# From batch 3 on, q and k of a head on 64 partitions instead of 32: loaded twice, one element apart

## The chip, the cores and the metric

The kernel runs on one NeuronCore of a Trainium2 chip. The metric is the device time of one execution in microseconds (us), lower is better. A core has five engines that run their own instruction streams: TensorE (PE, matmuls; PEld is its weight load), VectorE (DVE), ScalarE (ACT), GpSimd (POOL) and SyncE (SP). Transfers are issued from an engine's queue (here SP, POOL and once ACT) and carried out by 16 DMA engines.

## The reference

Inputs are q, k and v of shape (8, 8, 576, 64) (batch, head, position, head dimension), and two weight matrices, (512, 2048) and (2048, 512), all float32.

```python
def _attn_ref(q, k, v):
    factor, Sd, scale = 4, S // 4, 1.0 / np.sqrt(D)
    # pooled part: means over 4 positions, full softmax attention over 144 positions
    q_d, k_d, v_d = (t.reshape(B, H, Sd, 4, D).mean(axis=3) for t in (q, k, v))
    out_up = np.repeat(softmax(scale * q_d @ k_d.T) @ v_d, 4, axis=2)
    # local part: only |i - j| < 4
    mask = np.abs(pos[:, None] - pos[None, :]) < 4
    out_local = softmax(np.where(mask, scale * q @ k.T, -1e9)) @ v
    return out_up + out_local

def _moe_ref(x, w_in, w_out):            # x: 4608 tokens x 512
    h = x @ w_in
    return (h * sigmoid(1.702 * h)) @ w_out
```

The two parts of attention are added, the heads are laid side by side as 512 columns, and the result passes through the two matrix products with the activation between them.

## The kernel before

**Tiling.** The 4608 tokens are cut into 9 groups of 512 (`n_groups`). For a group g, `mm1` computes 16 blocks of 128 hidden units (`ffc`), each of four 512-column matmuls over the model dimension (`dmc`, one for each pair of heads; L806), followed by an activation on ScalarE (L817). `mm2` computes four blocks of 128 tokens, 16 matmuls of 512 columns each (L884), followed by a copy on ScalarE and a store (L869, L874). So a group has 64 + 64 large matmuls.

**Order.** The schedule is written by hand: each engine runs its instructions in program order. The attention of batch b = g + 1 is threaded into the matmuls of group g. `attention(b)` returns five steps, and `POS` says before which matmul each is put: numbers below 16 are blocks of mm1, later ones are matmuls of mm2 counted from 16. The steps are: the scores of quad 0 on TensorE, their exponentials and masks, the scores and exponentials of quad 1, and twice attn-times-v (`avx`) for four heads.

**Scores.** A quad is four heads. `load_1` loads q or k of a quad as 128 partitions x 1152 bf16 values (the DMA, issued on GpSimd, casts from float32); two buffers per name and quad (`bufs=2`). `prep_1` (L312) transposes in blocks of 32x32 on VectorE, with two bf16 values taken as one float32. So a head lies on 32 partitions, and its 64 dimensions are 32 pairs (index `a`). A score is the sum of two matmuls with 32 rows, a = 0 and a = 1, accumulated in PSUM. `scores_mixed` issues per quad 80 local matmuls (L439: 64 keys by 60 queries) and 24 pooled ones through `scores_d` (L466: 64 keys by 144 queries), four at a time on the four row groups, on tiles of 32 rows by 64 columns. The pooled q and k (`qdT`, `kdT`) are sums of four positions: on GpSimd (`pool_qk`, two adds each, L343 and L347) or on VectorE (`reduce_qk`, one reduction, L331). Scores go to PSUM tiles PA (three of two banks each), exponentials to `es` and `ed` (L477, L503), and the local ones are multiplied by the band mask on VectorE (L511).

**The rest of attention.** `avx` works on 64x64 tiles, four abreast: L674 pooled, L696 local, each with denominators from a matrix of ones. ScalarE takes logarithms and an exponential for the reciprocal (L739 to L745), VectorE multiplies (L750), and the pooled part is added to xT on GpSimd for heads 0 to 3 and on VectorE for heads 4 to 7 (L766).

**Around it, per group.** Before mm1 of group g (batch b = g + 1, b below 8) this is issued; every engine picks out its own part:

```python
            load_v4(b)              # SP: v as rows of four positions, 12 transfers
            prep_qk(b, 0)           # DVE: transposes k and q of quad 0
            pool_qk(b, 0)           # POOL: their pooled sums
            if b + 1 < B:
                for qd in range(NQ):
                    load_qk(b + 1, qd)   # POOL queue: four loads
            prep_v(b, nc.gpsimd)    # POOL: v to bf16 (L353)
            if b + 1 < B:
                load_v(b + 1)       # SP: ten transfers
            prep_qk(b, 1)           # DVE: quad 1
            ...
            prep_v4(b, nc.gpsimd)   # POOL: pooled v (L360, L363), from v4 to vd
```

In the place of the dots quad 1's pooled sums are made, for b = 2 on VectorE and for later batches on GpSimd. Batch 0 is done ahead of the groups with its own functions (`scores0`, `normalise0`, `transp_sum`), and batch 1 in group 0.

## Time and profile before

| | us |
|---|---|
| median of 3 runs (313.42 to 315.02) | 314.03 |
| the profiled execution, its own time | 312.69 |
| its span, from first to last instruction | 310.9 |
| TensorE busy | 299.7 |
| ScalarE busy | 203.4 |
| VectorE busy | 148.3 |
| GpSimd busy | 146.9 |
| local score matmuls L439, 1120 of them, mean 0.195 each | 15.4 busy |
| pooled score matmuls L466, 384 of them, mean 0.237 each | 12.3 busy |
| transposes L312, 32 of 128x576, mean 1.24 each | 39.7 busy |

The granted TensorE clock is 1.00 over the span. Busy time of an engine is the union of its instructions' time. Small matmuls overlap on TensorE, so their mean durations say little of what they cost: the distance between starts does. Some matmul records are missing from a trace, which shows as a gap of twice the usual distance. A line such as L439 is the line of the kernel before; "idle before" names what the engine waited for.

### The profile page before, as it was taken

What the parts mean: (1) busy time and instruction counts of PE and PEld (TensorE: products, weight loads), DVE (VectorE), ACT (ScalarE), POOL (GpSimd) and SP (SyncE); (2) the same over time, 40 slices, a digit from 0 to 9 for tenths busy, and PEclk for the clock granted to TensorE, in tenths of its full rate; (3) what the DMA queues carried; (4) which work ended last, traced back from release to release, by engine and by line L of the source; (5) the groups of instructions that cost most, each with busy time, mean ns of one, the idle gap of its engine ahead of it and who ended that gap; (6) DMA issues with size and microseconds to landing.
All of it is one profiled execution on the core that took longest, in us unless ns stands there. A gap on an engine that the chain in (4) does not pass through costs nothing.

```text
span 310.9 us, 9597 instructions
## 1 busy us (share of the span) xinstructions
PE 299.7 (96%) x4138; PEld 156.2 (50%) x4181; DVE 148.3 (48%) x304; ACT 203.4 (65%) x327; POOL 146.9 (47%) x169
## 2 busy tenths in 40 slices
PE   8899999999999999999999999999999999999995
PEld 3464555665544464455545554555455544444444
DVE  6984936851694159505970499038902760000000
ACT  4755766777858786768866885589558857216511
POOL 8542393394229933894369634983396110000000
PEclk9999999999999999999999999999999999999999
DMA  6999999899527942795159705981430110010011
GB/s 110 138 208 209 185 136 216 241 201 226 161 94 163 206 120 87 166 224 139 70 168 201 177 36 174 193 211 39 137 89 34 39 70 0 34 67 36 0 67 67
DMA packets 64042, 39.93 MB, mean 128 GB/s; under 512 B 44544, under 2 KB 54912, under 8 KB 64000
## 3 DMA queue, kind: packets, MB, share of 16 engines
q0 software_dynamic: 18784, 14.94, 32.9%
q1 hardware_dynamic: 45072, 24.32, 28.0%
q8 instruction: 32, 0.52, 0.7%
q14 instruction: 10, 0.08, 0.1%
q10 hardware_dynamic: 144, 0.07, 0.1%
HBM read 44.81 MB, written 9.44 MB: 174 GB/s over the span
## 4 chain that ended last, share of the span: by engine, by line
PE 91%; DMA 2%; issue 2%; POOL 2%; ACT 1%; DVE 1%; POOLq 0%; DVEq 0%; ACTq 0%
PE pm L884 36%; PE pm L806 24%; PE pa L806 16%; PE pa L439 3%; DMA vb<-in_v_dram 2%; PE pa L884 2%; PE pa L696 2%; PE pa L674 2%; PE pa L466 2%; PE pm L899 1%; POOL vb L260 1%; PE pa L609 1%; PE pa L567 1%; PE pa L597 0%; POOL kb L218 0%
## 5 line engine op out<-in xcount | busy, mean ns | idle before, releaser
L884 PE MATMUL pm<-w_out_bf,gT 128*128 128x512 bf16 x503 | 114.6, 379 | 3.4 <-issue 3.2
L806 PEld LDWEIGHTS <-w_in_bf 128*128 128x128 bf16 x603 | 58.3, 98 | 63.8 <-issue 0.3
L806 PE MATMUL pm<-xT,w_in_bf 128*128 128x512 bf16 (+1 forms) x342 | 86.9, 375 | 0.6
L884 PEld LDWEIGHTS <-gT 128*128 128x128 bf16 x560 | 52.7, 98 | 62.4 <-issue 0.6
L817 ACT ACTIVATE gT<-pm 128x512 bf16<-128x512 f32 x88 | 52.7, 603 | 41.0 <-PE pm L806 41.0
L806 PE MATMUL pa<-xT,w_in_bf 128*128 128x512 bf16 (+1 forms) x245 | 59.0, 361 | 0.3
L511 DVE TENSOR_TENSOR es<-es,mask 128x600 bf16<-128x600 bf16 x28 | 17.2, 651 | 85.6 <-ACT es L477 85.5
L869 ACT ACTIVATE osb<-pm 128x512 f32<-128x512 f32 (+2 forms) x35 | 20.3, 583 | 30.5 <-PE pm L884 25.1
L817 ACT ACTIVATE gT<-pa 128x512 bf16<-128x512 f32 x56 | 32.1, 608 | 6.3 <-PE pa L806 6.3
L766 POOL TENSOR_TENSOR xT<-xT,od 128x576 bf16<-128x576 bf16 x12 | 15.4, 1280 | 40.0 <-DVE xT L750 40.0
L750 DVE TENSOR_TENSOR xT<-n,l 128x285 bf16<-128x285 f32 (+1 forms) x96 | 28.1, 366 | 0.0
L343 POOL TENSOR_TENSOR pq<-kT 128x576 f32<-128x576 bf16 x11 | 12.8, 1160 | 30.4 <-DVE kT L312 30.4
L871 DVE TENSOR_SCALAR osb<-pm 128x128 f32<-128x128 f32 x1 | 0.3, 291 | 53.8 <-ACT osb L869 53.8
L360 POOL TENSOR_TENSOR pq<-v 112x512 f32<-112x512 f32 x18 | 23.7, 1317 | 3.9 <-DMA v<-in_v_dram 3.9
L312 DVE STREAM_TRANSPOSE kT<-kb 128x576 f32<-128x576 f32 x16 | 19.9, 1244 | 4.4 <-DMA kb<-in_k_dram 4.4
L312 DVE STREAM_TRANSPOSE qT<-qb 128x576 f32<-128x576 f32 x16 | 19.8, 1238 | 0.3
L503 ACT ACTIVATE ed<-pa 128x864 bf16<-128x864 f32 x16 | 14.3, 894 | 7.2 <-PE pa L466 7.2
L477 ACT ACTIVATE es<-pa 128x600 bf16<-128x600 f32 x28 | 17.2, 669 | 0.1
L745 ACT ACTIVATE l<-l 128x1440 f32<-128x1440 f32 x12 | 16.8, 1404 | 0.4
L740 DVE COPY n<-pa 128x492 f32<-128x492 f32 x24 | 15.0, 665 | 2.7 <-ACT l L739 2.0
L739 ACT ACTIVATE l<-pa 128x492 f32<-128x492 f32 x24 | 12.6, 578 | 4.6 <-PE pa L696 3.7
L439 PE MATMUL pa<-qT,kT 32*64 32x60 bf16 x1120 | 15.4, 195 | 0.0
(132 smaller groups left out, 355.0 us busy)
## 6 DMA issues: line engine op xcount, KB each, us to landing
out_dram<-osb SPq DMA_DIRECT2D x34, 256.0 KB, 2.2
vf<-in_v_dram SPq DMA_DIRECT2D x60, 128.0 KB, 4.9
v<-in_v_dram SPq DMA_DIRECT2D x72, 96.0 KB, 3.1
kb<-in_k_dram POOLq DMA_DIRECT2D x16, 288.0 KB, 6.5
qb<-in_q_dram POOLq DMA_DIRECT2D x16, 288.0 KB, 8.6
w_out_bf<-in_moe_w_out_dram POOLq DMA_DIRECT2D x4, 512.0 KB, 13.2
w_in_bf<-in_moe_w_in_dram POOLq DMA_DIRECT2D x2, 512.0 KB, 6.8
w_in_bf<-in_moe_w_in_dram POOLq DMA_DIRECT2D x1, 1024.0 KB, 12.2
```

What stands on the lines that cost most here:

```text
L312: nc.vector.transpose(out=t32.rearrange("p (i c) -> p c i", c=18), in_=store[b, qd].bitcast(FP32).rearrange("p (c d) -> p c d", c=18),)
L360: eng.tensor_tensor(out=t1[0:112], in0=x[:, :, 0:2, :], in1=x[:, :, 2:4, :], op=ALU.add)
L439: nc.tensor.matmul(P[1 + r // 2][64 * par : 64 * par + 64, r % 2, 60 * i : 60 * i + 60], lhsT=kT[b, qd][rows, k0 : k0 + 64, a], rhs=qT[b, ...
L477: nc.scalar.activation(out=es[2 * qd + u][:, :, 0:300], in_=sp[u][:, :, 0:300], func=AF.Exp, scale=inv_sqrt_d,)
L511: nc.vector.tensor_tensor(out=ev, in0=ev, in1=mask, op=ALU.mult)
L745: nc.scalar.activation(out=l, in_=l, func=AF.Exp, scale=-1.0)
L750: nc.vector.tensor_tensor(out=out, in0=sub(n, *part), in1=sub(l, *part), op=ALU.mult)
L766: eng.tensor_tensor(out=xs, in0=xs, in1=sub(od[:, u, :], 0, (1, SD), (0, 4)), op=ALU.add)
L806: nc.tensor.matmul(acc[:, c : c + n], lhsT=w_in_bf[:, dmc, ffc * 128 : (ffc + 1) * 128], rhs=xT[dmc][:, g * TG + c : g * TG + c + n], star ...
L817: nc.scalar.activation(out=gT[:, ffc, :], in_=acc, func=AF.Silu, scale=GELU_SCALE)
L869: eng.activation(out=osb, in_=ap, func=AF.Copy, scale=1.0 / GELU_SCALE)
L884: nc.tensor.matmul(ops[t], lhsT=gT[:, ffc, t * 128 : (t + 1) * 128], rhs=w_out_bf[:, ffc, :], start=(ffc == 0), stop=(ffc == n_ffc - 1),)
```

## The change

From batch 3 on (`WIDE = 3`) the four heads of a quad are taken as two pairs u, each on 64 partitions. The 2 x 576 x 64 values of a pair are 32 rows of 2304. A load puts them on 32 partitions, and once more on the next 32, beginning one element later (so 2303 values each). The transposition by float32 pairs is the same operation, with 36 instead of 18 blocks per row. Of every pair only its first value is used: the first copy gives the even dimensions, the second the odd ones. So a head's 64 dimensions lie on 64 partitions, a score is one matmul of 64 rows, on 64x64 tiles (`scores_wide`), and a quad has 40 local and 12 pooled matmuls.

With it come: one raw tile of 2304 columns per name and quad, whose halves serve as the two buffers of the batches before 3, and which is a single buffer from batch 3 on; tiles of twice the length for the transposed q and k, in whose second halves batch 0's y and the helper dm0 lie; the pooled sums of quad 1 on VectorE in every batch from 2 on; the loads of quad 1 issued after `prep_v4`; steps 3 to 5 of the attention one matmul later; and in group 8 eight matmuls of 512 columns issued as two of 256.

```diff
...
     n_dmc = d_model // 128
     n_ffc = d_ff // 128
     n_groups = B * S // TG
+    WIDE = 3
     inv_sqrt_d = 1.0 / math.sqrt(D)
     KSTART = (0, 56)
     QSTART = (0, 60)
...
         ez.append(t[:, 0:2560].rearrange("p (u j i c) -> p u j i c", u=2, j=2, c=128))
     v4 = persist.tile([128, 3, HP, 4 * D], FP32, name="v4")
     kdT = [persist.tile([128, 160, 2], BF16, name=f"kdT{i}") for i in range(NQ)]
+    raw = {
+        (n, qd): persist.tile([128, 2304], BF16, name=f"{n}b{qd}")
+        for qd in range(NQ) for n in "kq"
+    }
 
     PA = [psum.tile([128, 2, 512], FP32, name=f"pa{i}") for i in range(3)]
     PM = [psum.tile([128, 512], FP32, name=f"pm{i}") for i in range(2)]
...
     PSEL_AT = {(i, kc): 48 * kc - 114 * i // 4 + (EVEN + 37 if i % 2 else 18)
                for i, kc in ((0, 0), (1, 0), (1, 1), (2, 1), (3, 1), (3, 2), (4, 2))}
 
-    dm0 = consts.tile([128, Q0], FP32, name="dm0")
     dm = consts.tile([128, 60], FP32, name="dm")
     di = consts.tile([128, 128], FP32, name="di")
     dr = consts.tile([128, 1], FP32, name="dr")
...
         for t in ez:
             nc.vector.memset(t.rearrange("p u j i c -> p (u j i) c")[:, :, Q0:128], 1.0)
         for t in kT0:
-            nc.vector.memset(t[:, S:, :], 0.0)
+            nc.vector.memset(t[:, S : S + 8, :], 0.0)
         nc.vector.memset(vbs[0][96:128, 4, :, 0:D], 0.0)
         make_bias()
         make_off()
...
     qf, kf, vf = {}, {}, {}
 
     def load_1(name, src, store, b, qd):
-        t = ldp.tile(
-            [128, 1152], BF16, name=f"{name}b{qd}", tag=f"{name}b{qd}", bufs=2
-        )
+        t = raw[name, qd]
+        if b >= WIDE:
+            store[b, qd] = t
+            for u in range(2):
+                nc.gpsimd.dma_start(
+                    out=t[64 * u : 64 * u + 64, 0:2303],
+                    in_=bass.AP(
+                        tensor=src.tensor, offset=src[b, 4 * qd + 2 * u].offset,
+                        ap=[[1, 2], [2304, 32], [1, 2303]],
+                    ),
+                )
+            return
+        store[b, qd] = t = t[:, 1152 * (b % 2) : 1152 * (b % 2) + 1152]
         nc.gpsimd.dma_start(
             out=t,
             in_=bass.AP(
...
                 ap=[[1152, 128], [1, 1152]],
             ),
         )
-        store[b, qd] = t
 
     def load_qk(b, qd):
         load_1("k", k, kf, b, qd)
...
 
     qT, kT, qdT = {}, {}, {}
 
-    def new_T(name, qd):
-        n = S + 8 if name == "k" else S
-        return work.tile([128, n, 2], BF16, name=f"{name}T{qd}", tag=f"{name}T{qd}", bufs=1)
-
-    kT0 = [new_T("k", qd) for qd in range(NQ)]
+    rows_T = {"k": 2 * S + 8, "q": 2 * S}
+    wholeT = {
+        (n, qd): persist.tile([128, rows_T[n], 2], BF16, name=f"{n}T{qd}")
+        for qd in range(NQ) for n in "kq"
+    }
+    kT0 = [wholeT["k", qd] for qd in range(NQ)]
+    dm0 = wholeT["q", 1].rearrange("p t a -> p (t a)")[:, 4 * S - 2 * Q0 :].bitcast(FP32)
 
     def prep_1(name, b, qd):
         store, dst = {"k": (kf, kT), "q": (qf, qT)}[name]
-        tt = kT0[qd] if name == "k" and b == 0 else new_T(name, qd)
-        t32 = tt[:, 0:S, :].rearrange("p t a -> p (t a)").bitcast(FP32)
+        tt = wholeT[name, qd]
+        n, c = (2 * S, 36) if b >= WIDE else (S, 18)
+        t32 = tt[:, 0:n, :].rearrange("p t a -> p (t a)").bitcast(FP32)
         nc.vector.transpose(
-            out=t32.rearrange("p (i c) -> p c i", c=18),
-            in_=store[b, qd].bitcast(FP32).rearrange("p (c d) -> p c d", c=18),
+            out=t32.rearrange("p (i c) -> p c i", c=c),
+            in_=store[b, qd].bitcast(FP32).rearrange("p (c d) -> p c d", c=c),
         )
         dst[b, qd] = tt
+        if b >= WIDE:
+            dst[b, qd] = tt[:, 0:n, :].rearrange("p (x t) a -> p x t a", x=2)[:, :, :, 0]
 
     def prep_qk(b, qd):
         prep_1("k", b, qd)
...
         qdT[b, qd] = t
         return t
 
+    def by_head(t):
+        return t.rearrange("p t a -> p (t a)").rearrange("p (x t) -> p x t", x=2)
+
+    kd2 = [by_head(t) for t in kdT]
+    qd2 = {}
+
+    def pooled(b, qd, name):
+        t = kdT[qd][:, 0:SD, :] if name == "k" else new_qdT(b, qd)
+        if b < WIDE:
+            return t
+        if name == "k":
+            return kd2[qd][:, :, 0:SD]
+        qd2[b, qd] = by_head(t)
+        return qd2[b, qd]
+
     def reduce_qk(b, qd, name):
-        t = kdT[qd][:, 0:SD, :] if name == "k" else new_qdT(b, qd)
+        t = pooled(b, qd, name)
         src = (kT if name == "k" else qT)[b, qd]
+        if b >= WIDE:
+            src = src.rearrange("p x (j f) -> p x j f", f=4)
+        else:
+            src = src[:, 0:S, :].rearrange("p (j f) a -> p j a f", f=4)
         with nc.allow_low_precision("the sum is rounded once, as the pairwise one is"):
             nc.vector.tensor_reduce(
-                out=t, in_=src[:, 0:S, :].rearrange("p (j f) a -> p j a f", f=4),
-                axis=mybir.AxisListType.X, op=ALU.add,
-            )
-
-    def pool_qk(b, qd, names="kq"):
+                out=t, in_=src, axis=mybir.AxisListType.X, op=ALU.add,
+            )
+
+    def pool_qk(b, qd):
         for name, src in (("k", kT), ("q", qT)):
-            if name not in names:
-                continue
-            sv = src[b, qd][:, 0:S, :].rearrange("p (j f) a -> p j f a", f=4)
             t1 = work.tile([128, SD * 4], FP32, name="pq", tag="pq")
-            t1 = t1.rearrange("p (j f a) -> p j f a", f=2, a=2)
+            if b >= WIDE:
+                sv = src[b, qd].rearrange("p x (j f) -> p x j f", f=4)
+                t1 = t1.rearrange("p (x j f) -> p x j f", f=2, x=2)
+                two, one = (sv[:, :, :, 0:2], sv[:, :, :, 2:4]), (t1[:, :, :, 0], t1[:, :, :, 1])
+            else:
+                sv = src[b, qd][:, 0:S, :].rearrange("p (j f) a -> p j f a", f=4)
+                t1 = t1.rearrange("p (j f a) -> p j f a", f=2, a=2)
+                two, one = (sv[:, :, 0:2, :], sv[:, :, 2:4, :]), (t1[:, :, 0, :], t1[:, :, 1, :])
+            nc.gpsimd.tensor_tensor(out=t1, in0=two[0], in1=two[1], op=ALU.add)
             nc.gpsimd.tensor_tensor(
-                out=t1, in0=sv[:, :, 0:2, :], in1=sv[:, :, 2:4, :], op=ALU.add
-            )
-            dst = kdT[qd][:, 0:SD, :] if name == "k" else new_qdT(b, qd)
-            nc.gpsimd.tensor_tensor(
-                out=dst, in0=t1[:, :, 0, :], in1=t1[:, :, 1, :], op=ALU.add
+                out=pooled(b, qd, name), in0=one[0], in1=one[1], op=ALU.add
             )
 
     def prep_v(b, eng, i=slice(0, 5), h=slice(0, H)):
...
                 local(n // 2, n % 2, 0)
         return P[0], P[1:3]
 
+    def scores_wide(b, qd, P):
+        def local(n, us):
+            x, i = n % 2, n // 2
+            for u, par in us:
+                rows = slice(64 * u, 64 * u + 64)
+                k0 = 114 * i + KSTART[par]
+                q0 = 114 * i + QSTART[par]
+                nc.tensor.matmul(
+                    P[1 + u][64 * par : 64 * par + 64, x, 60 * i : 60 * i + 60],
+                    lhsT=kT[b, qd][rows, x, k0 : k0 + 64],
+                    rhs=qT[b, qd][rows, x, q0 : q0 + 60],
+                    start=True, stop=True,
+                    tile_position=(64 * u, 64 * par),
+                )
+
+        def down(n):
+            x, kc = n % 2, n // 2
+            for u in range(2):
+                rows = slice(64 * u, 64 * u + 64)
+                nc.tensor.matmul(
+                    P[0][rows, x, SD * kc : SD * kc + SD],
+                    lhsT=kd2[qd][rows, x, 48 * kc : 48 * kc + 64],
+                    rhs=qd2[b, qd][rows, x, :],
+                    start=True, stop=True,
+                    tile_position=(64 * u, 64 * u),
+                )
+
+        straight, across = ((0, 0), (1, 1)), ((0, 1), (1, 0))
+
+        def plain(ns):
+            for n in ns:
+                local(n, straight + across)
+
+        if qd:
+            plain(range(4))
+        for n in range(6):
+            down(n)
+            local(n + (4 if qd else 0), across + straight)
+        if not qd:
+            plain(range(6, 10))
+        return P[0], P[1:3]
+
     def scores_d(b, qd, sd=None, rounds=range(6)):
         bank = [sd[:, u, :] for u in range(2)]
         for n in rounds:
...
                         tile_position=(64 * j, 0),
                     )
 
-    def y_tiles0():
+    def y_tiles0(hp):
+        t = wholeT["kq"[hp // 2], hp % 2][:, S + 8 : 2 * S, :].rearrange("p t a -> p (t a)")
         return (
-            work.tile([128, 7, 2, D], BF16, name="y", tag="y", bufs=4),
+            t[:, 0 : 14 * D].rearrange("p (c x d) -> p c x d", c=7, x=2),
             work.tile([128, 2, 7, 1], FP32, name="rc0", tag="rc0", bufs=4),
         )
 
...
 
         def s_pe(qd):
             P = PB if b == 1 else PA
-            st["d", qd], st["s", qd] = scores_mixed(b, qd, P)
+            scores = scores_wide if b >= WIDE else scores_mixed
+            st["d", qd], st["s", qd] = scores(b, qd, P)
 
         def s_act(qd):
             if qd == 0:
...
         return first + [lambda: avx(b, (0, 1)), lambda: avx(b, (2, 3))]
 
     def hps_mm(g, ffc, dmc, acc):
-        n = TG // 2 if g == 1 and dmc and ffc < 9 else TG
+        halved = (g == 1 and dmc and ffc < 9) or (g == 8 and dmc > 1 and ffc < 4)
+        n = TG // 2 if halved else TG
         for c in range(0, TG, n):
             nc.tensor.matmul(
                 acc[:, c : c + n],
...
         for f in steps.get(n, ()):
             f()
 
-    POS = [12, 16, 34, 42, 53]
+    POS = [12, 16, 35, 43, 54]
     POS_0 = [16, 18, 28, 40, 49, 58, 67]
     VDP_0 = 36
 
...
     exp0(1)
     for hp in range(4):
         o[hp] = PB[hp % 3]
-        y[hp] = y_tiles0()
+        y[hp] = y_tiles0(hp)
     prep_vd_pe(
         0, PM[0], (0, 1), eng=nc.vector,
         between=lambda kc, i: av_local0(0, o[0], range(3 * ((kc, i) == (1, 3)))),
...
             prep_qk(b, 0)
             pool_qk(b, 0)
             if b + 1 < B:
-                for qd in range(NQ):
-                    load_qk(b + 1, qd)
+                load_qk(b + 1, 0)
             prep_v(b, nc.gpsimd)
             if b + 1 < B:
                 load_v(b + 1)
             prep_qk(b, 1)
-            if b == 2:
-                reduce_qk(b, 1, "k")
-                reduce_qk(b, 1, "q")
-            else:
-                pool_qk(b, 1)
+            reduce_qk(b, 1, "k")
+            reduce_qk(b, 1, "q")
             prep_v4(b, nc.gpsimd)
+            if b + 1 < B:
+                load_qk(b + 1, 1)
         steps = {}
         if b < B:
             for n, f in zip(POS if g else POS_0, attention(b)):
```

## The prediction

> **What bounds the kernel now.** I read the page's busy shares and its chain first, then the sums by group of tokens, then the order of time on TensorE, and at last VectorE and GpSimd around one burst of scores.
>
> ```profile
> PE 299.7 (96%) x4138; PEld 156.2 (50%) x4181; DVE 148.3 (48%) x304; ACT 203.4 (65%) x327; POOL 146.9 (47%) x169
> PE 91%; DMA 2%; issue 2%; POOL 2%; ACT 1%; DVE 1%; POOLq 0%; DVEq 0%; ACTq 0%
> ```
> TensorE is on 91% of the chain; the other engines are about half busy. The windows, by group (g=3, then g=7, which has no attention in it):
>
> ```profile
> 122.30:154.70 32.40, 31.82 (x509) 16.29 (x513) 17.47 (x35) 23.59 (x36) 20.31 (x21) 1.00 0.63 149
> 251.80:279.50 27.70, 27.54 (x127) 12.59 (x129) 2.10 (x6) 11.41 (x20) 0.00 (x0) 1.00 0.12 45
> ```
> The clock is 1.00 in both. A group with attention is about 4.65 us longer than one without: that is the price of a batch's scores and its attn-times-v on TensorE, with nothing idle beside it. DMA is busy 0.63 of such a group. The timeline of TensorE in g=3 (start, length, line, count):
>
> ```profile
> 130.94 1.89 PE L806 MATMUL pm<-xT,w_in_bf 128*128 128x512 bf16 x8
> 132.76 0.26 PE L466 MATMUL pa<-qdT,kdT 32*64 32x144 bf16 x4
> ...
> 133.36 0.51 PE L439 MATMUL pa<-qT,kT 32*64 32x60 bf16 x40
> 133.80 3.63 PE L806 MATMUL pm<-xT,w_in_bf 128*128 128x512 bf16 x15
> ...
> 144.16 0.26 PE L674 MATMUL pa<-ed,vd 48*64 48x144 bf16 x4
> 144.25 0.23 PE L674 MATMUL pa<-ed,ones 48*64 48x144 bf16 x4
> 144.31 0.23 PE L674 MATMUL pa<-ed,vd 48*64 48x144 bf16 x4
> ...
> 144.79 0.27 PE L696 MATMUL pa<-es,vb 64*64 64x57 bf16 x12
> 144.89 0.20 PE L696 MATMUL pa<-es,ones 64*64 64x60 bf16 x4
> ```
> 512-column matmuls start 0.2155 us apart, so the eighth of the first row starts at 132.45. The next one starts at 133.80, so quad 0's burst costs 1.35 - 0.22 = 1.13 us: 0.918 from its first to its last start, the rest entering and leaving. Three things are to be seen here. Forty local matmuls, each with its weight load, start within 0.33 us: 8.3 ns a pair, whatever the tile. On 64x64 tiles, four matmuls of 144 columns take 62 to 66 ns together, so four tiles run abreast and a tile takes 144 columns in about 62 ns. Four of 57 columns take 33 ns, which is again 4 x 8.3.
>
> **Part by part.**
>
> *Fewer score matmuls.* A quad had 80 local and 24 pooled matmuls, and now has 40 and 12. A burst of 104 pairs at 8.3 ns is 0.87 us; the measured 0.918 is nearly that, so the burst is held by the rate at which pairs are issued. New burst: 52 pairs x 8.3 = 0.43 us by issue. But the columns that one tile sees do not shrink: tile (0,0) still takes 6 pooled matmuls of 144 columns and 10 local ones of 60. In `scores_wide` the pooled matmul and the straight local share a tile, in order: a round is 62 + about 28 = 90 to 92 ns (the 28 from 32 ns between two 60-column starts on one tile before, and 60/144 of 62 = 26). Six rounds are 0.55, and four plain rounds at 33 ns are 0.13: 0.68 us. The tile is now the bound, not the issue. The ten bursts of batches 3 to 7 took, by the trace's starts, 4.58 us (quad 0) and 4.70 us (quad 1: 0.91 each, 0.97 and 0.99 in g=4 and g=5), together 9.28. Ten at 0.68 are 6.8: **-2.48 us**. The bounds are 0.43 (issue alone: -5.0) and 0.918 (no shorter: 0). I take 0.68, because the attn-times-v rows show both limits at work. This lies wholly on the chain.
>
> *Eight 512-column matmuls of g=8 cut in halves.* The 32 halves at L899 take 3.51 us on the chain, 0.110 each, so a pair costs 0.219 against 0.2155: 8 x 0.004 = **+0.03 us**.
>
> *Bursts one matmul later.* It moves nothing in or out of TensorE. ScalarE needs about 4.2 us from the end of mm1 to the end of the pooled exponential that frees PA[0] (137.2 to 141.39); the new burst reaches its pooled matmuls 0.25 us sooner after its start, and 0.22 of that is given back. A wait of 0 to 0.1 us per quad 1 may remain (0 to 0.5 in all; I take 0). At the end of a group the last products come 0.22 us later: VectorE adds xT of heads 4 to 7 until 156.06 and 156.73, and mm1 of g=4, from 154.65 on, reads them 8 and 12 matmuls later, at 156.37 and 157.24. Of 0.31 us of cover 0.1 is left: zero, at worst 0.1 a group.
>
> *Transposes twice as wide, quad 1's pooling on VectorE.* The cover in question, VectorE first, then GpSimd, g=3:
>
> ```profile
> 124.29 1.25 DVE L312 STREAM_TRANSPOSE kT<-kb 128x576 f32<-128x576 f32 x1
> 125.39 1.24 DVE L312 STREAM_TRANSPOSE qT<-qb 128x576 f32<-128x576 f32 x1
> ```
> ```profile
> 125.62 1.15 POOL L343 TENSOR_TENSOR pq<-kT 128x576 f32<-128x576 bf16 x1 [5.30 <-DVE kT L312]
> 127.47 1.15 POOL L343 TENSOR_TENSOR pq<-qT 128x576 f32<-128x576 bf16 x1
> 128.70 0.67 POOL L347 TENSOR_TENSOR qdT<-pq 128x288 bf16<-128x288 f32 x1
> ```
> Counted from the start of mm1 (122.31), VectorE begins at +2.0, q0 is turned at +4.3, its pooling ends at +7.05, and the burst's pooled matmuls, which need it, start at +10.45: 3.4 us of cover. New transposes have twice the columns at 1.09 us per 576 (start to start), so 2.2 each; VectorE starts 0.22 later; q0 is turned at +6.65, and GpSimd's two adds (1.9 us, the element counts unchanged) end at +8.65. Cover left: 1.8 us, cost **0**. Behind these on VectorE stand k1 and q1 (+11.0), then two reduces of 1.3 us (L331 in the groups by form) to +13.6; the first mask, at +17.8, and quad 1's burst, at +18.9, come later. If the cover is gone, each us costs 1 us in five groups. No row shows a 1152-column transpose or these strides on GpSimd; bounds below.
>
> *GpSimd and its queue.* It loses quad 1's pooling (3.8 us) and gains four DMA issues of 0.57: prep_v4 ends at about +19.7 instead of +21.6, and the attn-times-v that waits for it starts at +21.85, where only 0.25 us had been left (143.92 to 144.165). A gain in cover, none in time. Quad 1's loads are issued behind prep_v4, at +20 to +22. In g=1 nothing moves ahead of prep_v4.
>
> *Loads.* They double: 20 loads of 288 KB become pairs of 288 KB.
>
> ```profile
> kb<-in_k_dram POOLq DMA_DIRECT2D x16, 288.0 KB, 6.5
> qb<-in_q_dram POOLq DMA_DIRECT2D x16, 288.0 KB, 8.6
> ```
> Four issued together in g=3 at 129.3 landed by 139.55, with about 14 of the 16 DMA engines busy on them (packets of 2304 B, 0.206 us each): 128 x 0.206 / 16 = 1.65 us of all engines per load. Four more per batch are 6.6 us, so the busy share of a group goes from 0.63 to about 0.83. Each half batch is now what a whole batch was, so some 10 us to land: quad 0 issued at +8.7, landed at +20, needed at the next group's +2 (+34.5); quad 1 issued at +20 to +22, landed at +32, needed at +39. The raw tile is single now, but its transposes are over before either issue. Cost **0** as long as the pairs spread over all engines as the 128-partition loads do; no row shows a load whose outermost count is 2.
>
> [...]
>
> **Sum.** Span 310.9 - 2.48 + 0.03 = 308.45; the profiled execution's 312.69 becomes 310.2. That execution lay 1.34 us under the median of the runs, 314.03, so the forecast for the median is 314.03 - 2.45 = **311.6 us** (-0.8%). Its own range is 310.6 (small extra saving) to 312.4 (0.1 us waits in five to six groups and a tile that changes hands more slowly).
>
> **Rivals.**
>
> *First: each wide load sits on two DMA engines.* Place: the v4 loads of g=1, which share the queue time with the first wide loads.
>
> ```profile
> 76.81 1.27 POOL L360 TENSOR_TENSOR pq<-v 112x512 f32<-112x512 f32 x1 [1.70 <-DMA v<-in_v_dram]
> 78.16 0.73 POOL L363 TENSOR_TENSOR vd<-pq 112x256 bf16<-112x256 f32 x1
> ```
> The last vd is ready at 78.89, 0.6 us before its first reader (79.47), because GpSimd waited for v4, whose packets alternate one to one with those of q and k. Four loads on two engines each would put 32 packets of twice the size (0.41 us) on eight engines, each followed by a v4 packet (0.055): 14.9 us from 65.5, the last 11 of 43 v4 packets after that, v4 landed at 81, vd at 83.5, a stall of 3.6 us once. Later groups have v4 landed earlier and hold. Time: 314.03 - 2.45 + 3.6 = 315.2. For it: an outermost count of 2. Against: all the loads that the trace shows fill 14 to 16 engines.
>
> *Second, slower: GpSimd hands q's pooled half over too late.* Place: the pooled matmuls of quad 0's burst, five groups. It decides once q0's transpose and pooling take more than 8.25 us from VectorE's start instead of 6.45. With GpSimd's adds at twice their time for the new strides (2.3 + 1.3 for k from +4.5, then for q to +11.8) TensorE waits 1.35 us, five times: 6.7 - 2.45 = +4.3, so 318.3. Against: L360 and L363, on other shapes, cost 2.6 and 3.0 ns a column where L343 and L347 cost 2.0 and 2.3; at 3.0 throughout the pooling would end at +9.7, still in time.
>
> *Third: the bursts do not shorten.* If the shared tile costs more between matmuls than 28 ns, say a round of 130 ns, a burst is 0.91 as before, and the time stays 314.0. For it: the same columns per tile. Against: the attn-times-v rows, where tiles change weights at 33 ns.
>
> *Fourth: issue alone binds.* Then 0.43 a burst: 9.28 - 4.33 = 4.95 saved, 309.1. [...]
>
> **How the numbers follow.** Forecast 0.55, first rival 0.13, second 0.12, third 0.12, fourth 0.08. Half a percent, about what a measurement of this kernel can tell from no change, is 1.6 us. Faster by more than that: the forecast, the fourth, and a little of the third: 0.64. Within it: the first at its price, most of the third: 0.20. Slower: the second and the first where more than its one stall comes late: 0.16. The range takes in the fourth (309.1) and reaches past the first to 316.0; left out are most of the second and what lies under the fourth.
>
> **What would show it.** Right: in g=2 to g=6 the gap between the 512-column matmuls around a burst falls from 1.13 to about 0.9 us; L439 and L466 keep counts only of batches 1 and 2, the new line's 64x64 matmuls start in rounds of about 90 ns; transposes of 128x1152 near 2.3 us; no wait on pq or qdT before the burst. A group's length falls from 32.35 to about 31.85. Wrong: a wait of L466's successor on GpSimd at +10.5, a longer wait of L360 on v in g=1, loads of kb or qb that take over 20 us to land, or rounds of 130 ns.

## The result and the profile after

The changed kernel takes 366.11 us (median of 4 runs, 361.39 to 368.99) against 313.73 for the kernel before: a ratio of 1.1612, 95% interval [1.1492, 1.1731]. One of the four executions, that of 368.99, ran in a slower state, and the ratio leaves it out. The forecast was 311.6 us, in a range of 309.1 to 316.0. The profiled execution, the fastest of the four, took 361.39 us; its span is 359.6. In line numbers of the changed kernel L888 is mm1, L966 mm2, L503 and L515 the new local and pooled scores, L754 and L776 attn-times-v, L397 and L400 the pooled v (from v4 to vd), L285 the load of v4, L251 that of vf, L951 the copy to the output buffer `osb`, L956 its store.

From the page: busy shares, granted clock in 40 slices, shares of the chain.

```profile
PE 315.8 (88%) x3669; PEld 158.1 (44%) x3669; DVE 182.4 (51%) x314; ACT 203.9 (57%) x327; POOL 146.0 (41%) x169
PEclk9999999997887999679996999979999999999999
DMA 37%; PE 36%; DVE 8%; POOL 6%; ACT 5%; SPq 3%; issue 2%; POOLq 0%; DVEq 0%; ACTq 0%
```
TensorE's share of the chain fell from 91% to 36%; transfers now carry 37%. The clock row has dips, which it did not have before. The bursts themselves did what the sum said (timeline of TensorE, quad 0 in g=2: start, length, line, count):

```profile
117.76 1.67 PE L888 MATMUL pm<-xT,w_in_bf 128*128 128x512 bf16 x7
119.36 0.25 PE L515 MATMUL pa<-qdT,kdT 64*64 64x144 bf16 x2
119.37 0.31 PE L503 MATMUL pa<-qT,kT 64*64 64x60 bf16 x8
119.48 0.23 PE L515 MATMUL pa<-qdT,kdT 64*64 64x144 bf16 x2
...
119.89 0.35 PE L503 MATMUL pa<-qT,kT 64*64 64x60 bf16 x16
120.17 3.63 PE L888 MATMUL pm<-xT,w_in_bf 128*128 128x512 bf16 x16
```
Pooled pairs start 0.09 to 0.12 us apart, and first to last start is 0.688 us (119.364 to 120.051; before 0.918). The gap that the burst makes between large matmuls is 0.905 us instead of 1.135: 0.23 saved, ten times, 2.3 us.

The loss is elsewhere. The DMA issues (last column: median us to landing) and the queue of GpSimd's transfers:

```profile
out_dram<-osb SPq DMA_DIRECT2D x34, 256.0 KB, 5.2
v<-in_v_dram SPq DMA_DIRECT2D x72, 96.0 KB, 9.8
kb<-in_k_dram POOLq DMA_DIRECT2D x20, 287.9 KB, 16.6
qb<-in_q_dram POOLq DMA_DIRECT2D x20, 287.9 KB, 18.0
```
```profile
q0 software_dynamic: 37024, 20.90, 40.4%
```
The same rows of the kernel before, where k and q took 6.5 and 8.6 us:

```profile
out_dram<-osb SPq DMA_DIRECT2D x34, 256.0 KB, 2.2
v<-in_v_dram SPq DMA_DIRECT2D x72, 96.0 KB, 3.1
```
```profile
q0 software_dynamic: 18784, 14.94, 32.9%
```
The wide loads need 16.6 and 18.0 us to land, and everything beside them is later too: v4 9.8 instead of 3.1, stores 5.2 instead of 2.2. While all four loads of a quad are in flight and little else is (94 to 100 us), 8.0 of the 16 DMA engines are busy with their 4606-byte packets: two engines a load. q0 also has 19,168 packets of 4 bytes, 928 before. The increase fits 40 loads x 14 other engines x 32 = 17,920, and 320 for the 20 DMAs more.

What waits for that, from the waits (us in total, times, longest):

```profile
POOL pq L397 <- DMA v<-in_v_dram: 48.3, 12, 11.9
ACT osb L951 <- DMA out_dram<-osb: 32.4, 4, 9.8
PE pm L888 <- ACT osb L951: 27.6, 5, 8.5
PEld L754 <- POOL vd L400: 9.9, 5, 6.0
```
There are two paths to TensorE. One is the foreseen one: v4 to vd to attn-times-v. The other is new, a chain through the output buffers; here at the end of g=1, SyncE's queue, then ScalarE, then TensorE:

```profile
72.03 17.90 SPq L251 DMA_DIRECT2D vf<-in_v_dram  x10
90.02 17.44 SPq L956 DMA_DIRECT2D out_dram<-osb  x4
```
```profile
106.50 0.60 ACT L951 ACTIVATE osb<-pm 128x512 f32<-128x512 f32 x1 [7.51 <-DMA out_dram<-osb]
```
```profile
100.32 0.59 PE L888 MATMUL pa<-xT,w_in_bf 128*128 128x512 bf16 x2
107.15 1.01 PE L888 MATMUL pm<-xT,w_in_bf 128*128 128x512 bf16 x2 [6.23 <-ACT osb L951]
```
The last vf loads and the four wide loads of quad 1 are issued together (87.9 to 90.6). The store of the group's first token block is issued behind them, at 90.02, and lands at 106.42. There are three output buffers; the fourth copy needs the first buffer back and waits until 106.50; the PSUM bank that it empties is the one that the next group's mm1 wants.

Against the profiled execution before, the span grew by 48.7 us. From the distances of starts: mm1 idle at the start of g=2 to g=5, 6.4 + 8.7 + 6.8 + 6.0 = 27.9 us; attn-times-v waiting for vd, 6.7 in g=1 (a gap of 7.91 instead of 1.18) and 1.2 in each of three later groups, with small ones 10.4; 55 large matmuls that start mostly 0.427 us apart instead of 0.2155, each time right behind one of these stalls of 6.0 to 8.7 us, 11.2 (the granted clock between 107.2 and 112.4 us is 0.50); group 0 and the head of g=1, where the waits for w_out differ from execution to execution, 2.1; the bursts -2.3. Together 49.3.

### The profile page after: what moved, and what is told of

It is laid out like the page before. It is cut to its first block, busy times and chain, and to the rows that moved or that the text cites. A ratio compares the mean times of both kernels' runs of the same rounds, so it can differ in the third digit from the quotient of the medians.

```text
span 359.6 us, 8630 instructions
## 1 busy us (share of the span) xinstructions
PE 315.8 (88%) x3669; PEld 158.1 (44%) x3669; DVE 182.4 (51%) x314; ACT 203.9 (57%) x327; POOL 146.0 (41%) x169
## 4 chain that ended last, share of the span: by engine, by line
DMA 37%; PE 36%; DVE 8%; POOL 6%; ACT 5%; SPq 3%; issue 2%; POOLq 0%; DVEq 0%; ACTq 0%
DMA v<-in_v_dram 19%; PE pm L966 16%; PE pm L888 10%; DMA w_out_bf<-in_moe_w_out_dram 8%; DMA out_dram<-osb 7%; PE pa L888 6%; SPq L285 3%; DVE xT L830 3%; DMA vb<-in_v_dram 2%; POOL pq L397 2%; DMA w_in_bf<-in_moe_w_in_dram 2%; PE pa L776 1%; DVE kT L328 1%; DVE qT L328 1%; PE pa L754 1%
## 5 line engine op out<-in xcount | busy, mean ns | idle before, releaser
L966 PE MATMUL pm<-w_out_bf,gT 128*128 128x512 bf16 x528 | 120.7, 382 | 0.6 <-DMA w_out_bf<-in_moe_w_out_dram 0.6
L888 PE MATMUL pm<-xT,w_in_bf 128*128 128x512 bf16 (+1 forms) x362 | 94.5, 389 | 27.7 <-ACT osb L951 27.6
L888 PEld LDWEIGHTS <-w_in_bf 128*128 128x128 bf16 x611 | 61.4, 102 | 99.0 <-issue 42.6
L966 PEld LDWEIGHTS <-gT 128*128 128x128 bf16 x560 | 53.0, 98 | 63.4 <-issue 2.2
L888 PE MATMUL pa<-xT,w_in_bf 128*128 128x512 bf16 (+1 forms) x249 | 64.9, 382 | 0.0
L951 ACT ACTIVATE osb<-pm 128x512 f32<-128x512 f32 (+2 forms) x35 | 20.3, 582 | 57.2 <-DMA out_dram<-osb 32.4
L397 POOL TENSOR_TENSOR pq<-v 112x512 f32<-112x512 f32 x18 | 23.1, 1283 | 61.0 <-DMA v<-in_v_dram 48.3
L328 DVE STREAM_TRANSPOSE kT<-kb 128x1152 f32<-128x1152 f32 (+1 forms) x16 | 29.7, 1853 | 9.3 <-DMA kb<-in_k_dram 9.3
L328 DVE STREAM_TRANSPOSE qT<-qb 128x1152 f32<-128x1152 f32 (+1 forms) x16 | 29.7, 1857 | 3.2 <-DMA qb<-in_q_dram 3.1
L819 ACT ACTIVATE l<-pa 128x492 f32<-128x492 f32 x24 | 12.6, 578 | 16.6 <-PE pa L776 16.0
L383 POOL TENSOR_TENSOR pq<-kT 128x576 f32<-128x576 bf16 x6 | 6.9, 1146 | 35.2 <-DVE kT L328 28.9
L820 DVE COPY n<-pa 128x492 f32<-128x492 f32 x24 | 15.0, 665 | 11.8 <-ACT l L819 11.2
L400 POOL TENSOR_TENSOR vd<-pq 112x256 bf16<-112x256 f32 x18 | 14.3, 792 | 1.4
## 6 DMA issues: line engine op xcount, KB each, us to landing
kb<-in_k_dram POOLq DMA_DIRECT2D x20, 287.9 KB, 16.6
```

The costliest lines, as they stand in the source:

```text
L328: nc.vector.transpose(out=t32.rearrange("p (i c) -> p c i", c=c), in_=store[b, qd].bitcast(FP32).rearrange("p (c d) -> p c d", c=c),)
L397: eng.tensor_tensor(out=t1[0:112], in0=x[:, :, 0:2, :], in1=x[:, :, 2:4, :], op=ALU.add)
L820: nc.vector.tensor_copy(out=n[:, par, 0:RS], in_=mains(par)[:, 0, 0:RS])
L888: nc.tensor.matmul(acc[:, c : c + n], lhsT=w_in_bf[:, dmc, ffc * 128 : (ffc + 1) * 128], rhs=xT[dmc][:, g * TG + c : g * TG + c + n], star ...
L951: eng.activation(out=osb, in_=ap, func=AF.Copy, scale=1.0 / GELU_SCALE)
L966: nc.tensor.matmul(ops[t], lhsT=gT[:, ffc, t * 128 : (t + 1) * 128], rhs=w_out_bf[:, ffc, :], start=(ffc == 0), stop=(ffc == n_ffc - 1),)
```

## The experiments

Each diff shows the lines that matter; the kernel that it starts from is named. Times are medians; a ratio is to the kernel before in the same set of runs.

**1. The loads spread.** From the changed kernel: each wide load as two DMAs of 32 partitions, with an outermost count of 32. Nothing else is changed.

```diff
-            for u in range(2):
+            for r in range(4):
                 nc.gpsimd.dma_start(
-                    out=t[64 * u : 64 * u + 64, 0:2303],
+                    out=t[32 * r : 32 * r + 32, 0:2303],
...
-                        ap=[[1, 2], [2304, 32], [1, 2303]],
+                        offset=src[b, 4 * qd + r // 2 * 2].offset + r % 2,
+                        ap=[[2304, 32], [1, 2303]],
```


> The changed kernel, each wide load cut into two of 32 partitions, one for each of the two shifts, so that the outermost count of its source is 32 and not 2; bytes and everything else as in the change. Few engines (a load sits on as many DMA engines as its outermost count allows, and the stores and the v4 loads wait behind it): all 16 engines share the work, kb and qb land within 10 to 12 us, no store and no v4 load is late; 311 to 313 us, that is the sum of the prediction, with GpSimd issuing 16 loads a batch instead of 8. Volume (twice the bytes are what delays the others): the bytes are the same, so some 355 to 366 us as in the change. Other edits (order of loads, moved pooling): also unchanged, some 360.

Measured: 320.07 us, 1.0178 [1.0151, 1.0204]. Of the 52 us 46 are gone: kb lands in 4.7 us, v4 in 2.6, stores in 2.5. The 17,920 packets of 4 bytes are gone too. Two of its issues:

```profile
v<-in_v_dram SPq DMA_DIRECT2D x72, 96.0 KB, 2.6
kb<-in_k_dram POOLq DMA_DIRECT2D x40, 143.9 KB, 4.7
```
So the two engines are the cause of the large loss. But 312 was expected, and it is 320. The good groups are 31.84 us long, as forecast. In three others TensorE stands still with no engine to release it, for instance (timeline of TensorE; L967 is mm2 here):

```profile
150.19 0.82 PE L967 MATMUL pm<-w_out_bf,gT 128*128 128x512 bf16 x3
153.07 2.10 PE L967 MATMUL pm<-w_out_bf,gT 128*128 128x512 bf16 x9 [2.06 <-issue]
```
The gaps cost 2.2, 3.2 and 2.2 us, with six half-rate matmuls behind the longest (1.2 us), and vd in g=1 costs 0.8. In each of the three a packet of 16 KB of instructions was under way (from 150.73, 184.61 and 219.96, about 0.95 us long), and TensorE resumed 1.2 to 1.4 us after it had landed. Wide loads and vf's 256-byte packets were in flight together then. That TensorE's instructions came late was the author's reading from here on ("late code" below); a count in the next section speaks for it.

**2. Two engines in the kernel before.** Only the source pattern of the narrow loads from batch 3 on has an outermost count of 2 (the second half takes the data of other heads).

```diff
-                ap=[[1152, 128], [1, 1152]],
+                ap=([[36864, 2], [1152, 64]] if b >= 3 else [[1152, 128]]) + [[1, 1152]],
```


> The kernel before, with one edit: from batch 3 on the source of a load is written as 2 x 64 rows instead of 128 (the second 64 partitions take heads 1 and 2 of the quad instead of 2 and 3, so that the two counts can't be merged into one). Bytes, number of loads and their order are those of before. Few engines: every such load takes 64 packets of 0.206 us on each of two engines, 13.2 us and more to land, 8 engines busy for the four of a batch, filler packets of 4 bytes on the other 14; half of what the change puts there, so between 316 and 340 us. Volume: nothing is doubled, 314 us. Other edits: none is made, 314 us.

Measured: 318.52 us, 1.0170 [1.0122, 1.0218]. Its issues:

```profile
kb<-in_k_dram POOLq DMA_DIRECT2D x16, 288.0 KB, 15.5
qb<-in_q_dram POOLq DMA_DIRECT2D x16, 288.0 KB, 16.0
```
The landing times are nearly those of the changed kernel, with q0's 4-byte packets up by 17,920 (which fits 20 loads, 64 for each of the 14 other engines). The pattern alone makes the loads slow, without wide tiles or new bytes. What it costs is less sure: of the 5.9 us that the span of the profiled execution grew, 3.0 lie in g=2 to g=5, and as much ahead of g=1, where no such load has been issued yet (g=1 starts at 60.4 us, in all other kernels here between 57.4 and 59.1). So with half the bytes the pattern costs about 3 us.

**3. Everything but the wide form.** The changed kernel with `WIDE = 8`, so that no batch is wide: order of the loads, places of the bursts, pooling on VectorE and halved matmuls stay.

```diff
-    WIDE = 3
+    WIDE = 8
```


> The changed kernel with WIDE = 8, so that no batch is wide: narrow loads, transposes and scores as before, but with the rest of the change (loads of quad 1 behind prep_v4, pooling of quad 1 on VectorE, later bursts, halves in group 8, the tiles laid over each other). Few engines, and volume: 314 us, within 0.5 of before. Other edits: 320 us or more.

Measured: 314.53 us, 1.0042 [1.0012, 1.0071]. The rest of the change costs about 1 us: attn-times-v of heads 4 to 7 has 0.75, 0.15 and 0.2 us more in three groups, again with no engine to release it.

**4. A fourth output buffer.** The changed kernel with four `osb` buffers (paid for with one `pq` buffer instead of two).

```diff
-                osb = moe_sb.tile([128, n], FP32, name="osb", tag=f"osb{n}", bufs=3)
+                osb = moe_sb.tile([128, n], FP32, name="osb", tag=f"osb{n}", bufs=4 if n == d_model else 3)
```


> The changed kernel with four output buffers of 512 columns instead of three (the place is taken from the second buffer of GpSimd's scratch tile pq). Wide loads stay on two engines each. If the late stores that hold an output buffer, and with it ScalarE, PSUM and the start of mm1, make the greater part of the loss (four stalls of 6.2 to 8.9 us, and the lower clock behind each): 325 to 340 us. If the late v4 loads are the true bound and the stores only show it: 355 to 366 us, with the waits moved to attn-times-v on vd.

Measured: 351.6 us, 1.1219 [1.118, 1.1258], between the two forecasts. The wait on the stores has left the list, and the other path has grown (waits):

```profile
POOL pq L397 <- DMA v<-in_v_dram: 41.9, 9, 7.4
PEld L754 <- POOL vd L400: 30.6, 8, 6.0
```
Attn-times-v of heads 0 to 3 now waits 6.8, 6.6, 7.1, 3.9 and 8.7 us, in all five groups. The two late paths lie side by side: with the wait on the stores gone, 38 of the 52 us remain. What the stores would cost alone is not shown.

**5. Quad 1's loads later.** From experiment 1: they are issued behind the xT adds of heads 0 to 3, not behind prep_v4.

```diff
             prep_v4(b, nc.gpsimd)
-            if b + 1 < B:
-                load_qk(b + 1, 1)
...
+            elif b + 1 < B:
+                steps[POS[3]].append(lambda b=b: load_qk(b + 1, 1))
```


> e1_spread with quad 1's loads issued later: behind the adds to xT of heads 0 to 3 instead of behind prep_v4, some 8 us later in the group, so that they no longer run while TensorE goes through the two attn-times-v bursts. In e1_spread TensorE stood still there three times for 2 to 3 us without waiting for another engine, each time until a 16 KB packet of the instruction queue had come in. Late code (TensorE's own instructions come in behind the wide loads): these stalls go, groups of 31.85 us, 311 to 312.5 us. Volume (the doubled bytes cost e1_spread its time wherever they lie): 318 to 321 us. Late data (quad 1's transposes then wait for kb): 314 to 318 us, with a wait of quad 1's burst on kdT or qdT.

Measured: 316.59 us, 1.0069 [1.0038, 1.0100]. One gap without a releaser is left (0.67 us). In their place v4, now issued beside these loads, is late, and attn-times-v of heads 0 to 3 waits 1.4, 0.8, 1.8, 1.5 and 0.2 us for vd.

**6. The old order of the loads.** From experiment 3: quad 1's narrow loads back ahead of prep_v.

```diff
                 load_qk(b + 1, 0)
+                load_qk(b + 1, 1)
...
-            if b + 1 < B:
-                load_qk(b + 1, 1)
```


> e3_no_wide (nothing wide) with quad 1's narrow loads back ahead of prep_v, beside quad 0's. In e3_no_wide the attn-times-v bursts of heads 4 to 7 took 0.75, 0.15 and 0.2 us longer in three groups. Late code: these go with the loads, and the time falls by about 1 us, to 313.5. Other edits (pooling on VectorE, bursts later): it stays at 314.5.

Measured: 313.98 us, 1.0006 [0.9990, 1.0023]. With nothing wide and the loads early the time is that of the kernel before.

**7. Only quad 0 wide.** From experiment 1, with quad 1 narrow and all loads ahead of prep_v (the tests `b >= WIDE` become `b >= WIDE and not qd`).

```diff
                 load_qk(b + 1, 0)
+                load_qk(b + 1, 1)
...
-            if b + 1 < B:
-                load_qk(b + 1, 1)
```


> e1_spread with quad 0 alone wide; quad 1 is loaded and scored as before, its loads ahead of prep_v beside quad 0's. Half the bursts are shorter: 5 x 0.23 = 1.2 us less than before. Late code: nothing big is in flight during attn-times-v, so 312.7 us. Volume: half of e1_spread's loss stays, 315 to 317 us.

Measured: 321.05 us, 1.0253 [1.0217, 1.0289], outside both. In g=1 attn-times-v of heads 0 to 3 waits 2.6 us for vd, because GpSimd waits for v4. In the later groups vd costs 0.3 us at most, and four gaps without a releaser come back, about 4 us in all. GpSimd in g=1, then TensorE in g=2 (L398 is the pooled v, L777 attn-times-v here):

```profile
81.20 1.55 POOL L398 TENSOR_TENSOR pq<-v 112x512 f32<-112x512 f32 x1 [2.79 <-DMA v<-in_v_dram]
```
```profile
116.26 0.19 PE L777 MATMUL pa<-es,vb 64*64 64x57 bf16 x2
117.79 0.21 PE L777 MATMUL pa<-es,vb 64*64 64x57 bf16 x2 [1.34 <-issue]
```
No wide load was in flight in this gap (the last packet had come at 111.4 us), but vf's packets were, from 112.9 to 121.5. Ten load issues of about 0.5 us now stand on GpSimd ahead of prep_v. The loads of vf start only when prep_v has read its tile (the cast ends at 143.37 in g=3, the first load is issued at 143.40), so vf's packets now run into attn-times-v. Neither theory had counted the issues.

**8. The bursts back in their old places.** From experiment 5.

```diff
-    POS = [12, 16, 35, 43, 54]
+    POS = [12, 16, 34, 42, 53]
```


> e5_late with steps 3 to 5 of the attention at their old places, one matmul earlier. The prediction's step: quad 1's burst reaches PA[0] 0.25 us sooner after its start than before, so without the shift it waits for ScalarE up to 0.25 us in each of five groups: 0.5 to 1.2 us more than e5_late. If the shift does nothing: the same as e5_late within 0.3 us.

Measured: 316.85 us, 1.0099 [1.0075, 1.0124]. Quad 1's burst takes 0.067 us more in each group; the time can't be told from experiment 5's. One matmul later is worth a third of a us at most.

**9. The same bytes in narrow loads.** The kernel before, with the four loads of the next batch issued a second time behind prep_v4 (into the same tiles, g=1 to g=5).

```diff
             prep_v4(b, nc.gpsimd)
+            if 2 <= b < B - 1:
+                for qd in range(NQ):
+                    for n, src, st in (("k", k, kf), ("q", q, qf)):
+                        nc.gpsimd.dma_start(out=st[b + 1, qd], in_=bass.AP(
+                            tensor=src.tensor, offset=src[b + 1, 4 * qd].offset,
+                            ap=[[1152, 128], [1, 1152]]))
```


> The kernel before with one addition: in groups 1 to 5 the four narrow loads of the next batch are issued a second time behind prep_v4, into the same tiles with the same data. That puts on all 16 engines, at the time of the attn-times-v bursts, the bytes that quad 1's wide loads put there in e1_spread (4 x 8 packets of 0.206 us on each engine), and nothing else is changed. Late code (TensorE's instructions come in behind these packets): stalls of TensorE of 2 to 3 us that no engine's work ends, in some of five groups, 317 to 323 us. If the stalls of e1_spread came from the wide form itself: 314 us.

Measured: 314.50 us, 1.0020 [0.9998, 1.0043]. No gap appears. Late code by the mere amount loaded is refuted. These second loads were issued when vf had nearly landed, and ran without vf's packets beside them.

**10. A third of the pooled v on VectorE.** From experiment 5, so that vd is ready sooner.

```diff
         for kc in range(3):
+            eng = nc.vector if kc == 0 else first
```


> e5_late with the first of prep_v4's three chunks added on VectorE instead of GpSimd. In e5_late the code stalls were gone, and attn-times-v of heads 0 to 3 waited 0.2 to 1.8 us a group for vd, since GpSimd issues eight loads of 0.5 us ahead of it and v4 lands late. Two microseconds less on GpSimd: those waits shrink to the part that v4's landing sets; 313 to 315.5 us. If v4 alone sets them: as e5_late, 316.5.

Measured: 315.17 us, 1.0047 [1.0027, 1.0068]. Attn-times-v still waits 1.6, 0.5, 0.7 and 0.8 us in g=2 to g=5: v4 itself is late, not the work on it.

**11. v4 a group earlier.** From experiment 10: the next batch's v4 loads are issued behind attn-times-v of heads 0 to 3, ahead of quad 1's wide loads.

```diff
-            load_v4(b)
+            if b == 2:
+                load_v4(b)
...
-                steps[POS[3]].append(lambda b=b: load_qk(b + 1, 1))
+                steps[POS[3]].append(lambda b=b: (load_v4(b + 1), load_qk(b + 1, 1)))
```


> e9b_chunk with the v4 loads of the next batch issued behind attn-times-v of heads 0 to 3, some 7 us earlier and ahead of quad 1's wide loads, instead of at the start of the next group. If late vd was all that was left: no wait for v4, groups of 31.85 us, 311 to 312.5 us, less than both kernels. If the small v4 packets now delay TensorE's code instead: stalls without a releaser in attn-times-v, 314 to 318 us.

Measured: 312.90 us, 0.9968 [0.9949, 0.9987]: 0.3% less than the kernel before. One wait is left, 1.78 us in g=1, where v4 is still loaded at the head of the group.

**12. Wide loads only when vf has landed.** From experiment 1: a copy of one column of vf into the tile holds the loads of quad 1 back.

```diff
             if b + 1 < B:
+                nc.gpsimd.tensor_copy(out=raw["k", 1][:, 0:1], in_=vf[b + 1][:, 4, 0, 0:1])
                 load_qk(b + 1, 1)
```


> The loads spread over all engines (32 partitions a DMA), and ahead of quad 1's eight loads, behind prep_v4, GpSimd copies one column of the next batch's vf tile, so these loads are issued only when the last of vf has landed (some 2 us later than in the kernel with the loads spread, where they began at 145.0 while vf's 256-byte packets ran until 154). The amount loaded is the same. Theory: what made TensorE's instructions late was vf and the wide loads in flight together; then the three gaps of 2 to 3 us with no engine to release them are gone, the time is 312.5 to 315.5 us. Rival: the wide loads' packets alone make the instructions late; then a gap of 2 us or more remains in at least two groups, and the time is 318 to 321 us.

Measured: 321.17 us, 1.0239 [1.0194, 1.0283]: the rival's time, by another mechanism. The gaps in attn-times-v and in mm2 behind it are gone but for one of 0.5 us. In their place mm1 begins late in every group; GpSimd's timeline and TensorE's at the end of g=3:

```profile
153.46 0.53 POOL L1130 CAST kb<-vf 128x1 bf16<-128x1 f32 x1 [5.61 <-DMA vf<-in_v_dram]
154.28 1.99 POOL L223 DMA_DIRECT2D kb<-in_k_dram  x4 [0.29 <-POOL kb L1130]
156.26 1.94 POOL L223 DMA_DIRECT2D qb<-in_q_dram  x4
158.21 2.39 POOL L847 TENSOR_TENSOR xT<-xT,od 128x576 bf16<-128x576 bf16 x2
```
```profile
159.49 0.38 PE L889 MATMUL pm<-xT,w_in_bf 128*128 128x512 bf16 x1 [0.76 <-POOL xT L847]
160.65 0.38 PE L889 MATMUL pm<-xT,w_in_bf 128*128 128x512 bf16 x1 [0.78 <-POOL xT L847]
```
The gate holds GpSimd's queue for 5.6 us, and the xT adds stand behind it. Two steps of 1.14 and 1.16 us instead of 0.2155 cost 1.9 us, and the group lasts 33.8 instead of 31.84. The expectation had left out what is queued behind the gate.

**13. v4 of batch 2 a group earlier as well.** From experiment 11.

```diff
-            if b == 2:
-                load_v4(b)
...
+                steps.setdefault(POS_0[-1], []).append(lambda: load_v4(2))
```


> The kernel with the v4 loads issued early, and those of batch 2 issued in the group before (behind attn-times-v's last step of batch 1) in place of the head of group 1. The only wait left in that kernel was 1.78 us on vd in group 1, where v4 was loaded beside quad 0's wide loads (issued 63 to 71, landed 68 to 80 us). If those loads set it, it is gone and the time is 310.5 to 312.0 us; if another wait stands behind it, or the earlier loads delay the vf or weight loads of group 0, 312.5 to 314 us.

Measured: 312.03 us, 0.9936 [0.9916, 0.9956], the lowest median of all. Its window of g=3 (columns as in the windows before) and two of its issues:

```profile
123.86:155.70 31.84, 31.84 (x410) 15.75 (x408) 27.45 (x40) 23.58 (x36) 20.62 (x28) 1.00 0.87 190
```
```profile
v<-in_v_dram SPq DMA_DIRECT2D x72, 96.0 KB, 3.6
kb<-in_k_dram POOLq DMA_DIRECT2D x40, 143.9 KB, 4.8
```
TensorE is busy through the whole window, with DMA at 0.87. Only 0.3 and 0.1 us are left, in attn-times-v of heads 4 to 7 in two groups.

## Why the prediction was wrong, step by step

**The failed step is "Loads ... Cost 0 as long as the pairs spread over all engines".** They did not spread. The condition was named, and no row of the kernel before settled it: two engines a load was the first rival's guess, from the count alone. The runs show it for this case: with an outermost count of 2, 8.0 engines were busy for four loads, and with the same count on other data (experiment 2) the loads landed in 15.5 and 16.0 us; with 32 (experiment 1) kb landed in 4.7 us, without the 17,920 packets of 4 bytes. The reason given against the first rival, that all the loads of the trace fill 14 to 16 engines, was no evidence: the patterns of those loads have outermost counts of 48 to 128.

**The first rival came, and its price was wrong by a factor of 15.** "A stall of 3.6 us once" (4.0 by its own 83.5 and 79.47) was 6.7 in g=1: the last vd came at 87.98, not 83.5. "Later groups have v4 landed earlier and hold" was false, as experiment 4 shows: without the wait on the stores vd is 4 to 9 us late in each of the five groups. And two terms were missing altogether. One is the stores: the prediction followed q, k and v through the slowed queues, but not the output, which shares the engines and whose three buffers hand the delay to mm1 (27.9 us). The other is the rate behind a long stall: 55 matmuls at 0.427 us (11.2 us). The upper end of the range stood on this price, and the chance of 0.13 was too low for a condition that no row could settle. One of its signs was set too high as well: the loads landed in 16.6 and 18.0 us, not in over 20.

**Right: the bursts.** Forecast 0.68 us by tile (0,0), measured 0.688; forecast -2.48, measured -2.3. g=6, which loads nothing for a next batch, is 31.84 us long in the changed kernel, where 31.85 was forecast. Third and fourth rival, 0.91 and 0.43 a burst, are out. That the shared tile sets the time rests on the rounds of 0.09 to 0.12 us; no run changes the columns of a tile.

**Right: GpSimd's strides and the wider transposes.** Their cover held: no burst waits for the pooled q or k. The 128x1152 transposes start 2.1 us apart, where 2.2 was taken. The second rival is out.

**Off: "GpSimd and its queue ... a gain in cover, none in time".** With the loads spread they need twice the DMAs, eight issues of 0.5 us a quad. Whether these stand ahead of prep_v (experiment 7), beside v4's transfers (5) or behind a gate (12) decides over up to 2.6 us in a group. Only with v4 moved too (11, 13) does the forecast's mechanism show in the time: -2.0 us, where -2.45 was forecast for the change as it is.

**Late code: the count that speaks for it.** A weight load goes with each matmul (3669 of each on the page of the changed kernel). Counted in the traces, the gaps without a releaser come after TensorE's weight load 2143, 2527 and 2911 in experiment 1, after 1759 in 3, after 2527 in 5 and in 12, and after 1631, 1759, 2143 and 3039 in 7. Each of these numbers is 95 more than a multiple of 128, though the places in the schedule differ. There is one 16 KB packet of instructions for every 131 weight loads (28 for 3669 in the changed kernel, 32 for 4181 in the kernel before). That one portion of TensorE's code ended at these places, and that the next was not there yet, is the author's reading of the counts and of the packets that landed 1.2 to 1.4 us before TensorE resumed in experiment 1; no row shows it.

**What was in flight then: vf's packets, and with loads of q and k beside them the instruction packet came latest.** TensorE's instructions are the same in experiments 1 and 13. Take the three stretches of 128 weight loads, 3.8 to 4.4 us long, at whose ends experiment 1 stopped. In 1 the packet began to move 4.0 to 4.5 us after the start of the stretch, with vf's and the wide loads' packets in flight. In 13 it began after 1.3 to 1.6 us, with mostly vf's. The wide form is not needed: in the three groups of 3 that lost time, narrow loads beside vf gave 3.5 to 4.1 us. In three of the four gaps of 7, with mostly vf's packets in flight, it was 1.5 to 2.2 us (3.3 in the fourth), but TensorE ran through the stretch in 3.2 to 3.5. The mere amount loaded does not do it (9: 314.50 us, no gap). Where the packet waits is open.

## What to carry to other kernels

When a load's pattern is changed, look at how many DMA engines are busy while it is in flight: here 8.0 of 16 for four loads with an outermost count of 2, and a count of 32 instead, with the same bytes, took 46 of 52 lost us back. If a transfer becomes slow, price everything that shares its engines and queues, the output stores and their buffers too, in every group, not only the wait with the least cover. And in moving an issue or a wait on a queue, list what stands behind it: experiments 7 and 12 lost their gain there.

## What the runs showed of the hardware that was not expected

- The loads on two engines came with packets of 4 bytes: 17,920 more on q0 in the changed kernel and in experiment 2, which fits 32 and 64 a load for each of the other 14 engines. With an outermost count of 32 (experiment 1) they were gone.
- After mm1 stood for 6.0 to 8.7 us, large matmuls started 0.427 us apart for 11 to 13 of them, then at 0.2155 again; between 107.2 and 112.4 us, behind the first of these stalls, the granted clock was 0.50. In experiment 1 a stop of 2.8 us idle was followed by six of them, stops of 2.0 and 2.1 by none.
- In experiment 1 TensorE stood three times for 2.0 to 2.8 us idle with no engine to release it, while loads of vf, q and k ran; the profile calls it "issue". The stops came around attn-times-v, where TensorE goes through 128 weight loads in 3.2 to 5.8 us; with 512-column matmuls alone it would take 128 x 0.2155 = 27.6.
